# Attention in front of a squared-ReLU layer: another step order for the periods without conversions, and query and key loads taken from a list

## The chip, the cores and the metric

The kernel runs on one core of one Trainium2 chip. The metric is device time in microseconds (us) of one execution, as the median of several runs. Beside the runs there is one profiled execution with a trace of every instruction on TensorE (PE, its weight loads are PEld), VectorE (DVE), ScalarE (ACT), GpSimd (POOL) and the sequencer that issues most transfers (SP). Line numbers such as L453 are those of the kernel before.

## The reference

```python
scores = (q @ k.T) / 8                                # 8 batches, 8 heads, 576 x 576, head size 64
thresh = max(scores, axis=-1) - tau
scores = where(scores >= thresh, scores, -1e9)
attn   = exp(scores - max(scores)); attn = attn / (sum(attn) + 1e-9)
x      = (attn @ v) laid out as (8 * 576, 8 * 64)     # 4608 tokens x 512
h      = maximum(x @ w_in, 0)                         # 512 -> 2048
out    = (h * h) @ w_out                              # 2048 -> 512
```

`q`, `k`, `v` and `tau` are 32-bit floats. `w_in` and `w_out` arrive as 64-bit floats and are turned into 32-bit ones by the kernel itself, in integer arithmetic on ACT, POOL and DVE.

## The kernel before

**Stages.** The attention of all heads comes first (about the first 510 us of the span), then nine passes of the hidden layer, then the output layer. The two layers use a scheme of block sums (seven products for eight, twice nested), whose sums of weight blocks are made by POOL during the attention. The change touches the attention alone.

**Pairs, units and periods.** Two heads make a pair; there are 32 pairs. A unit is a block of 128 query rows of a pair (four per pair), or the last 64 rows of two pairs together; there are 144 units. A period p works on the two units A = 2p and B = 2p + 1 with their softmax; 72 periods hold the work and a few before and after fill and drain the pipeline. What belongs to one pair of units is spread over several periods, so that every engine has something to do.

**The steps** (names as in the order lists; `period`, L623, makes them):

- `T` transposes a pair's queries or keys on PE (L399); `eT` takes them out of PSUM on ACT (L404, L412) and then asks for the loads of a later pair (`ask_ahead`).
- `SA`, `SB` are the products of queries with 512 keys for units A and B (L435, 64x512), `RA`, `RB` the products with the last 64 keys (L435, 64x64).
- `topA0` to `topB1` find the row maxima of one head each on DVE and write the scores to SBUF (L453). `leastA`, `leastB` make the thresholds from them on POOL (L460). `powA0` to `powB1` are the exponentials on ACT (L463). `maskA0` to `maskB1` compare, multiply and sum on DVE (L468): two operands from SBUF, result to SBUF.
- `over` (POOL, L475) and `inv` (DVE, L478) make the inverse of the row sums; `Q` spreads it over 64 rows by small products on PE (L518).
- `V`, `W`, `U` transpose the weights of attention on PE (L381), nine chunks in three lots; `eV`, `eW`, `eU` take them out of PSUM on ACT (L526). `V` and `U` share one PSUM tile, `pt`; `W` and `Q` lie in two of the banks of `SB`.
- `PV` multiplies values with weights on PE (L535), into the banks that `SA` uses next. `x` takes the result out, half by ACT (L665), half by DVE (L667, in periods without conversions with the scaling). `xm` scales the other half on POOL (L677) and issues the stores of x (L581).
- `c1` to `c6` convert one chunk of weights, `fetch` loads one. `s1` and `s2` each take one step of a list of sums of weight blocks (and later of x for the first pass) on POOL: L122 or L125, one 128x512 operation, both inputs in SBUF.

**Orders.** An order is a string of step names, executed as program order by `run_period` (L731). A hyphen behind a name means that the step of the period before is meant, two hyphens of the one before that. Every engine executes its instructions in this order; semaphores alone tie the engines to each other. There are orders for periods 0 and 1 (`BEGIN_WITH`), one for the periods with conversions (`CONVERTING`, periods 2 to 34) and one for all others (`PLAIN`). `s1` acts from period 36 on, `s2` in periods 36 to 59 (its hyphen puts the instruction one period later).

**Order of one engine within a period without conversions, before** (lag within the pipeline left out):

- DVE: x, maskA0, then `inv`, then maskB0, topA0, topA1, maskB1, topB0, topB1, maskA1. In the trace's terms, from a first top: top, top, mask, top, top, mask, x, mask, inverse, mask.
- POOL: s2, xm, leastA, s1, leastB, over.

**Loads.** `load_q` issues two transfers of 128 KB for a pair, `load_k` seven smaller ones, all on SP (pair 0 in part on ACT). `ask_ahead` (L344) issues all of a pair's transfers at the place where `eT` stands, up to two pairs ahead. `load_v` issues one transfer per pair. `fetch` issues one transfer of 512 KB per chunk.

Of the kernel before, what the change touches and what calls it, by code (L numbers as in the profile page):

```python
# [48 lines left out]
def kernel(  # L49
# [25 lines left out]
    nc = tc.nc  # L75
    B, H, S, D = q.shape
    P = 128
# [212 lines left out]
    def load_q(i):  # L290
        b, hp = pairs[i]
        h = 2 * hp
        qn = sb.tile([P, FULL, P], FP32, tag="qn", bufs=2, name="qn")
        for j in range(2):
            nc.sync.dma_start(
                out=qn[:, :, ds(j * D, D)], in_=q[b, h + j, 0:MAIN, :].rearrange("(t p) d -> p t d", p=P)
            )
        loaded[i, 0] = qn

    def load_k(i):  # L300
        b, hp = pairs[i]
        h = 2 * hp
        kn = sb.tile([P, FULL, P], FP32, tag="kn", bufs=2, name="kn")
        rn = sb.tile([P, P], FP32, tag="rn", bufs=2, name="rn")
        for j in range(2):
            queue = nc.scalar if i == 0 and j == 0 else nc.sync
            keys = k[b, h + j, :, :].rearrange("(p c) d -> p c d", c=CH)
            for e in range(2):
                queue.dma_start(
                    out=kn[ds(e * HALF, HALF), :, ds(j * D, D)],  # L310
                    in_=keys[:, ds(e * FULL, FULL), :],
                )
# [3 lines left out]
            queue.dma_start(out=rn[REST:P, ds(j * D, D)], in_=keys[:, CH - 1, :])  # L316
        nc.sync.dma_start(
            out=rn[0:REST, :].rearrange("p (j d) -> p j d", j=2),
            in_=q[b, h : h + 2, MAIN:S, :].rearrange("j p d -> p j d"),
        )  # L320
        loaded[i, 1], loaded[i, 2] = kn, rn

    def load_v(i):
        b, hp = pairs[i]
# [66 lines left out]

    def turn(i, which, spots, other=None):

        nat, to = loaded.pop((i, which)), places(i)
        of = [nat[:, t, :] for t in range(FULL)] + ([loaded.pop((i, 2))] if which else [])
        for t, x in enumerate(of):
            for r, (spot, at) in enumerate(spots):
                rows = ds(r * HALF, HALF)
                made = nc.tensor.transpose(spot[:, ts(t, HALF)], x[rows, :], ident[rows, rows])  # L399
                touch("turns", made, at, BANK)  # L400
        half, kind = FULL * HALF, "turnedk" if which else "turnedq"

        def scaled(to, spot):
            touch(kind, nc.scalar.activation(out=to, in_=spot[0], func=AF.Identity, scale=qscale[:, :]), spot[1], BANK, i)  # L404
# [164 lines left out]
    def sums_due(p):  # L569

        return p > max(starts) + 2 and not converts(p)

    def sums_step():
        while summing and next(summing[0], 0) == 0:
            summing.popleft()

    def ask(every=True):

        while given:
            to, from_ = given.popleft()  # L580
# [11 lines left out]
    def begun(n):  # L592
        return starts.get(n)

    FIRST_PERIOD = -2
    PLAIN = """
        s2- PV-- x-- T-- V-- W-- c2 SA- c3- maskA0-- xm-- inv-- Q-- eT-- RB- maskB0-- topA0- c1- eV-- U-
        topA1- leastA- eW-- SB- powB1-- maskB1-- eU- RA topB0- c4 topB1- s1 powA1- leastB- maskA1- over- c5
        powA0- c6 powB0- fetch
    """.split()  # L600
    CONVERTING = """
        SB- c1 RA topB0- powA1- c2- topB1- PV- c5- powA0- maskA0- eT- leastB- over- V- x- T powB0- SA RB W-
        maskA1- c3 c4 inv- Q- c6- fetch topA0 eV- topA1 leastA U xm- maskB0- powB1- eW- eU maskB1- s1 s2
# [12 lines left out]

# [6 lines left out]
    def period(p):  # L623
# [48 lines left out]
        def given_out():  # L672
            if has(2 * m):
                x = late.pop("x")
                made = x[:, 0 : 1 + converts(p), :].rearrange("p j n -> p (j n)")
                scale = wT[m][:, ds(SCALE_AT * P, (1 + converts(p)) * P)]
                nc.gpsimd.tensor_tensor(out=made, in0=made, in1=scale, op=ALU.mult)  # L677
# [14 lines left out]
        def every(key):  # L692
# [13 lines left out]
            "s1": lambda: sums_due(p) and sums_step(), "s2": lambda: sums_due(p) and p < 60 and sums_step(), "fetch": lambda: fetch(begun(p + 2)),  # L706
            "next": lambda: fetch(begun(p + 3)),
        }
        steps["over"] = lambda: do(a, "over")
# [428 lines left out]
    with tc.manual_schedule():  # L1138
        with ExitStack() as stack:
            sc = stack.enter_context(tc.tile_pool(name="sc", bufs=1, space=PSUM)).tile([P, 6 * BANK], FP32, name="sc")  # L1140
            pt_pool = stack.enter_context(tc.tile_pool(name="pt", bufs=1, space=PSUM))

            def keep_busy(times, to=None):

                if to is None:
                    to = pt_pool.tile([P, 2, BANK], FP32, tag="pt", name="idle")[:, 0, 0:P]
                for _ in range(times):
                    nc.tensor.transpose(to, ident[:, :], ident[:, :])

            load_q(0)  # L1150
            load_k(0)
# [4 lines left out]
            ask_ahead(0, 1)  # L1156
            load_v(0)
# [204 lines left out]
```

## Time and profile before

| what | value |
|---|---|
| runs | 1315.05, 1312.97, 1312.98 us, median 1312.98 |
| profiled execution | 1310.12 us, span of its instructions 1308.3 us |
| PE busy | 1272.8 us (97% of the span) |
| DVE busy | 1015.0 us (78%) |
| ACT busy | 854.0 us (65%) |
| POOL busy | 1016.6 us (78%) |

The shares are means over three stages with different limits. In the page's 40 slices DVE is at nine tenths or more from the second slice to the fifteenth, and at five to eight tenths after the attention; ACT falls to two to six tenths there, and PE stays at nine tenths in nearly every slice. So what the attention costs is read from the attention's own stretch, and there from its two kinds of periods. A row of the trace's timeline gives start, duration, engine, line, operation, tiles and count; rows of one engine overlap where an instruction begins before the one ahead of it has drained, so that the step from start to start is what an instruction costs, and the duration is longer.

### The profile page before, as it was taken

To read this page: it belongs to the slowest core of one execution; us is meant where nothing else is said; L and a number is where in the kernel's file an instruction comes from. 1 tells how busy PE (TensorE), PEld (TensorE's weight loads), DVE (VectorE), ACT (ScalarE), POOL (GpSimd) and SP (SyncE) were. 2 spreads that over 40 slices of the span, in tenths; PEclk is the share of its full clock that TensorE was granted. 3 is DMA by queue.
4 is the path that set the end of the run, shared out by engine and by line. 5 is a ranking of instruction groups with operands and counts; after the bars stand their busy time and mean duration, and the time that the engine had idled before them with its cause. 6 is when DMAs were issued, how large, how long until landed. Compare 5 with 4: busy or idle time off the path is not lost.

```text
span 1308.3 us, 45977 instructions
## 1 busy us (share of the span) xinstructions
PE 1272.8 (97%) x18287; PEld 1104.7 (84%) x18287; DVE 1015.0 (78%) x2384; ACT 854.0 (65%) x1537; POOL 1016.6 (78%) x1070
## 2 busy tenths in 40 slices
PE   8999999999999999999999999999999999999998
PEld 5777766666666777988888888999999999999998
DVE  6999999999999996787886877867646654665463
ACT  6999999988888996576665866665524332433240
POOL 2999999887878652798897998858777777777775
PEclk8999999999999999999999999999999999999999
DMA  6555667443333322566767767779645234513511
GB/s 168 149 147 157 190 174 200 115 99 86 82 72 79 80 54 53 175 209 191 221 192 210 221 172 223 198 263 392 225 160 162 65 99 161 162 56 107 162 34 33
DMA packets 291415, 196.22 MB, mean 150 GB/s; under 512 B 100096, under 2 KB 252160, under 8 KB 291200
## 3 DMA queue, kind: packets, MB, share of 16 engines
q1 hardware_dynamic: 289888, 192.87, 50.9%
q8 instruction: 144, 2.36, 0.8%
q14 instruction: 71, 0.58, 0.1%
q10 hardware_dynamic: 1312, 0.41, 0.1%
HBM read 120.85 MB, written 72.35 MB: 148 GB/s over the span
## 4 chain that ended last, share of the span: by engine, by line
PE 71%; ACT 8%; DMA 6%; DVE 5%; issue 4%; POOL 4%; SPq 1%; DVEq 0%; POOLq 0%; ACTq 0%
PE po L1096 27%; PE ph L954 13%; PE ph L961 9%; PE sc L535 9%; PE sc L435 8%; ACT arena L526 3%; PE pt L381 2%; DVE arena L453 2%; ACT arena L463 2%; DMA g<-arena 2%; DMA arena<-xT 2%; DVE arena L468 1%; PE sc L399 1%; DVE arena L125 1%; DMA arena<-g 1%
## 5 line engine op out<-in xcount | busy, mean ns | idle before, releaser
L125 POOL TENSOR_TENSOR arena<-arena 128x512 f32<-128x512 f32 (+1 forms) x314 | 377.6, 1221 | 136.8 <-DVE arena L125 103.0
L1096 PE MATMUL po<-wall,arena 128*128 128x128 f32 x3528 | 395.1, 276 | 1.9 <-ACT arena L771 1.4
L1096 PEld LDWEIGHTS po<-wall,arena 128*128 128x128 f32 x3528 | 394.4, 192 | 2.5 <-ACT arena L771 1.8
L125 DVE TENSOR_TENSOR arena<-ph,arena 128x512 f32<-128x512 f32 x378 | 255.1, 689 | 78.8 <-PE ph L954 30.9
L122 POOL TENSOR_TENSOR arena<-arena 128x128 f32<-128x128 f32 (+1 forms) x322 | 264.8, 823 | 27.4 <-DMA arena<-w 11.6
L954 PE MATMUL ph<-arena,wall 128*128 128x256 f32 x1176 | 256.9, 381 | 3.1 <-DVE arena L125 2.7
L468 DVE SCALAR_TENSOR_TENSOR arena<-arena 128x576 f32<-128x576 f32 x288 | 256.4, 908 | 1.7 <-ACT arena L463 1.2
L954 PEld LDWEIGHTS ph<-arena,wall 128*128 128x128 f32 x1176 | 222.7, 190 | 37.0 <-DVE arena L125 7.9
L125 DVE TENSOR_TENSOR arena<-po,arena 128x128 f32<-128x128 f32 x378 | 108.3, 290 | 167.9 <-PE po L1096 163.6
L463 ACT ACTIVATE arena<-arena 128x576 f32<-128x576 f32 x288 | 215.6, 781 | 9.5 <-DVE arena L453 9.4
L810 ACT COPY c<-arena 128x512 f32<-128x512 f32 (+1 forms) x295 | 169.1, 578 | 74.5 <-DVE arena L122 35.8
L435 PE MATMUL sc<-arena 64*64 64x512 f32 (+1 forms) x2304 | 197.8, 423 | 16.8 <-DVE arena L453 8.6
L453 DVE TENSOR_SCALAR_CACHE_REDUCE arena<-sc 128x576 f32<-128x576 f32 x288 | 205.6, 750 | 8.8 <-PE sc L435 5.0
L460 POOL TENSOR_SCALAR arena<-arena,tau_p 128x2 f32<-128x2 f32 x144 | 102.2, 710 | 94.3 <-DVE arena L453 84.7
L122 DVE TENSOR_TENSOR arena<-arena,c 128x512 f32<-128x512 f32 x235 | 154.4, 666 | 13.3 <-ACT c L810 9.2
L535 PE MATMUL sc<-arena 64*64 64x128 f32 (+1 forms) x5760 | 163.0, 261 | 0.4 <-ACT arena L526 0.3
L435 PEld LDWEIGHTS sc<-arena 64*64 64x64 f32 x2304 | 75.7, 134 | 100.9 <-DVE arena L453 40.2
L526 ACT COPY arena<-pt 128x1024 f32<-128x1024 f32 x144 | 146.1, 1015 | 8.3 <-PE pt L381 7.7
L535 PEld LDWEIGHTS sc<-arena 64*64 64x64 f32 x5760 | 148.7, 134 | 1.4 <-ACT arena L526 0.7
L771 ACT COPY arena<-po 128x128 f32<-128x128 f32 x63 | 16.6, 264 | 186.4 <-PE po L1096 183.7
L961 PE MATMUL ph<-arena,wall 128*128 128x128 f32 x1176 | 132.0, 276 | 0.6 <-DVE arena L667 0.6
L961 PEld LDWEIGHTS ph<-arena,wall 128*128 128x128 f32 x1176 | 131.6, 192 | 0.9 <-issue 0.7
(54 smaller groups left out, 1153.6 us busy)
## 6 DMA issues: line engine op xcount, KB each, us to landing
arena<-g SPq DMA_DIRECT2D x144, 256.0 KB, 4.3
g<-arena SPq DMA_DIRECT2D x192, 128.0 KB, 2.9
w<-arena SPq DMA_DIRECT2D x60, 256.0 KB, 2.7
wall<-w SPq DMA_DIRECT2D x49, 256.0 KB, 5.2
g<-arena SPq DMA_DIRECT2D x48, 256.0 KB, 3.5
arena<-w SPq DMA_DIRECT2D x44, 256.0 KB, 3.3
arena<-in_v_dram SPq DMA_DIRECT2D x32, 288.0 KB, 4.1
out_dram<-arena SPq DMA_DIRECT2D x70, 128.0 KB, 2.8
```

What stands on the lines that cost most here:

```text
L122: e.tensor_tensor(out=out, in0=x, in1=y, op=ALU.subtract)
L125: e.tensor_tensor(out=out, in0=x, in1=y, op=ALU.add)
L435: made = nc.tensor.matmul(sc[at, ds(to, count)], lhs, kT[rows, ds(at_k, count)], start=True, stop=True)
L453: made = nc.vector.tensor_scalar(out=s[:, j, :], in0=sc[:, ds(at, S)], scalar1=1.0, scalar2=None, op0=ALU.mult, op1=ALU.min, accum_out=nmx ...
L463: nc.scalar.activation(out=w[:, :, j, :], in_=of(j), func=AF.Exp, bias=nmx[:, j : j + 1], scale=-1.0)
L468: nc.vector.scalar_tensor_tensor(out=w[:, :, j, :], in0=of(j), scalar=thr[:, j : j + 1], in1=w[:, :, j, :], op0=ALU.is_le, op1=ALU.mult, a ...
L526: touch("weights", nc.scalar.copy(joined(to), whole(pt, 0, count)), at, 2 * BANK, m)
L535: made = nc.tensor.matmul(sc[ds(u * D, D), ds(5 * j * BANK + row, count)], loaded_v[i][rows, (c - (u != j)) % CH, :], wT[m][rows, ds(weigh ...
L810: nc.scalar.copy(c, y)
L954: nc.tensor.matmul(to[:, 2 * j : 2 * j + 2, :], W_IN[m, k][:, ts(2 * h + j, P)], part_x(steps, k, m), start=(not more and j == 0), stop=Tr ...
L961: nc.tensor.matmul(to[:, j, :], W_IN[m, k][:, ts(j, P)], x, start=(not more and j == 0), stop=True, skip_group_check=True,)
L1096: nc.tensor.matmul(to, g[:, j, :], w[:, j, :], start=(not more and j == 0), stop=(j == 3), skip_group_check=True)
```

## The change

1. **A new `PLAIN` order.** The set of steps is the same, with `ahead` in front; the order and some lags differ.
2. **Query and key loads.** `load_q` and `load_k` become generators that yield after each transfer. `ask_ahead` appends them to a list `wanted`; the new step `ahead` issues three transfers from it (four in periods up to 1), and `given_out` (`xm`) issues two more, so five per period. `turn` takes from the list until its own pair's loads are out.
3. **Periods 0 and 1.** `ahead` is added. In period 1, `next`, which asks for the third chunk of weights, moves from the second place to the end.
4. `CONVERTING` gets `ahead` in front and is otherwise unchanged.

```diff
     def load_q(i):
         qn = sb.tile([P, FULL, P], FP32, tag="qn", bufs=2, name="qn")
+        loaded[i, 0] = qn
         for j in range(2):
-            nc.sync.dma_start(
+            yield nc.sync.dma_start(
...
     def ask_ahead(i, which):
         while asked[which] < min(len(pairs) - 1, i + (2 if i else 1)):
             asked[which] += 1
-            (load_k if which else load_q)(asked[which])
+            i_ = asked[which]
+            wanted.append((i_, which, (load_k if which else load_q)(i_)))
+
+    wanted = deque()
+
+    def ahead(count):
+        while wanted and count:
+            if next(wanted[0][2], 0) == 0:
+                wanted.popleft()
+            else:
+                count -= 1
...
     def turn(i, which, spots, other=None):
+        while any(x[0:2] == (i, which) for x in wanted):
+            ahead(1)
...
     PLAIN = """
-        s2- PV-- x-- T-- V-- W-- c2 SA- c3- maskA0-- xm-- inv-- Q-- eT-- RB- maskB0-- topA0- c1- eV-- U-
-        topA1- leastA- eW-- SB- powB1-- maskB1-- eU- RA topB0- c4 topB1- s1 powA1- leastB- maskA1- over- c5
-        powA0- c6 powB0- fetch
+        ahead PV-- RA- c2- c4- T- W-- U- c5- Q-- c1- maskB0-- x-- eT- SA- xm-- s1 maskB1-- RB- c3- eW-- SB-
+        eU- topA0- V- powA0- eV- topA1- topB0- topB1- powA1- powB0- over- leastA- powB1- inv- c6 maskA0- s2-
+        maskA1- leastB- fetch
     """.split()
...
     BEGIN_WITH = {
         0: """
-        SA RA RB SB fetch topA0 T topA1 leastA topB0 topB1 leastB powA0 powA1 eT powB0 powB1 maskA0 maskA1
-        maskB0 maskB1
+        SA RA RB SB fetch ahead topA0 T topA1 leastA topB0 topB1 leastB powA0 powA1 eT powB0 powB1 maskA0
+        maskA1 maskB0 maskB1
         """.split(),
         1: """
-        fetch next SA RA RB SB T eT over topA0 topA1 leastA inv V topB0 topB1 leastB powA0 powA1 eV W Q powB0 eW
-        maskA0 maskA1 powB1 maskB0 maskB1
+        fetch ahead SA RA RB SB T eT over topA0 topA1 leastA inv V topB0 topB1 leastB powA0 powA1 eV W Q
+        powB0 eW maskA0 maskA1 powB1 maskB0 maskB1 next
...
             ask(False)
+            ahead(2)
...
+            "ahead": lambda: ahead(3 if p > 1 else 4),
```

Engine by engine, a period of the new order from its first top on is, on DVE: topA0, topA1, topB0, topB1, inv, maskA0, maskA1, and then of the next period's list maskB0, x, maskB1. On POOL: over, leastA, s2, leastB, then xm, s1. On ACT: powA0, eV, powA1, powB0, powB1, then x, eT, eW, eU. On PE: SB, V, then PV, RA, T, W, U, Q, SA, RB. On SP at the start, the loads of the first two chunks now stand in front of the queries of pairs 2 and 3, and the third chunk behind them; before, the first chunk stood in front of these queries, and the second and third behind them.

More of the change, by code (lines that the diff above doesn't have):

```diff
@@ L293, in load_q @@
         qn = sb.tile([P, FULL, P], FP32, tag="qn", bufs=2, name="qn")
+        loaded[i, 0] = qn
         for j in range(2):
-            nc.sync.dma_start(
+            yield nc.sync.dma_start(
                 out=qn[:, :, ds(j * D, D)], in_=q[b, h + j, 0:MAIN, :].rearrange("(t p) d -> p t d", p=P)
             )
-        loaded[i, 0] = qn
     def load_k(i):
@@ L304, in load_k @@
         rn = sb.tile([P, P], FP32, tag="rn", bufs=2, name="rn")
+        loaded[i, 1], loaded[i, 2] = kn, rn
         for j in range(2):
@@ L308, in load_k @@
             for e in range(2):
-                queue.dma_start(
+                yield queue.dma_start(
                     out=kn[ds(e * HALF, HALF), :, ds(j * D, D)],
@@ L315, in load_k @@
                 nc.scalar.dma_start(out=tau_c[:, :], in_=wide)
-            queue.dma_start(out=rn[REST:P, ds(j * D, D)], in_=keys[:, CH - 1, :])
-        nc.sync.dma_start(
+            yield queue.dma_start(out=rn[REST:P, ds(j * D, D)], in_=keys[:, CH - 1, :])
+        yield nc.sync.dma_start(
             out=rn[0:REST, :].rearrange("p (j d) -> p j d", j=2),
@@ L320, in load_k @@
         )
-        loaded[i, 1], loaded[i, 2] = kn, rn
     def load_v(i):
@@ L596 @@
     PLAIN = """
-        s2- PV-- x-- T-- V-- W-- c2 SA- c3- maskA0-- xm-- inv-- Q-- eT-- RB- maskB0-- topA0- c1- eV-- U-
-        topA1- leastA- eW-- SB- powB1-- maskB1-- eU- RA topB0- c4 topB1- s1 powA1- leastB- maskA1- over- c5
-        powA0- c6 powB0- fetch
+        ahead PV-- RA- c2- c4- T- W-- U- c5- Q-- c1- maskB0-- x-- eT- SA- xm-- s1 maskB1-- RB- c3- eW-- SB-
+        eU- topA0- V- powA0- eV- topA1- topB0- topB1- powA1- powB0- over- leastA- powB1- inv- c6 maskA0- s2-
+        maskA1- leastB- fetch
     """.split()
     CONVERTING = """
-        SB- c1 RA topB0- powA1- c2- topB1- PV- c5- powA0- maskA0- eT- leastB- over- V- x- T powB0- SA RB W-
-        maskA1- c3 c4 inv- Q- c6- fetch topA0 eV- topA1 leastA U xm- maskB0- powB1- eW- eU maskB1- s1 s2
+        ahead SB- c1 RA topB0- powA1- c2- topB1- PV- c5- powA0- maskA0- eT- leastB- over- V- x- T powB0- SA
+        RB W- maskA1- c3 c4 inv- Q- c6- fetch topA0 eV- topA1 leastA U xm- maskB0- powB1- eW- eU maskB1- s1
+        s2
     """.split()
@@ L705, in period @@
             "c5": lambda: convert5(begun(p - 1)), "c6": lambda: convert6(begun(p - 1)),
-            "s1": lambda: sums_due(p) and sums_step(), "s2": lambda: sums_due(p) and p < 60 and sums_step(), "fetch": lambda: fetch(begun(p + 2)),
+            "s1": lambda: sums_due(p) and sums_step(), "s2": lambda: sums_due(p) and p < 60 and sums_step(), "ahead": lambda: ahead(3 if p > 1 else 4),
+            "fetch": lambda: fetch(begun(p + 2)),
             "next": lambda: fetch(begun(p + 3)),
@@ L1148, in keep_busy @@
                     nc.tensor.transpose(to, ident[:, :], ident[:, :])
-            load_q(0)
-            load_k(0)
+            for _ in load_q(0):
+                pass
+            for _ in load_k(0):
+                pass
             read_tau()
@@ L1156 @@
             ask_ahead(0, 1)
+            ahead(99)
             load_v(0)
```

## The prediction

> **What bounds the kernel now.** The page's shares are means over three stages, so I went to the windows of the two kinds of periods without conversions: with both sums of weight blocks (360 to 400 us) and after the second has ended (440 to 480). Columns: stretch, its length, busy us of PE, PEld, DVE, ACT, POOL, granted clock, DMA share, GB/s.
>
> ```profile
> 360.00:400.00 40.00, 37.62 (x980) 26.45 (x974) 39.43 (x103) 34.70 (x56) 32.04 (x34) 1.00 0.31 70
> 440.00:480.00 40.00, 39.99 (x1090) 30.42 (x1084) 39.31 (x113) 38.34 (x67) 23.81 (x31) 1.00 0.31 69
> ```
>
> DVE is busy for 98% of both. Yet the second stretch gets more done. The row maxima (four per period), by first and last start, tell the length of a period:
>
> ```profile
> L453 DVE TENSOR_SCALAR_CACHE_REDUCE arena<-sc x97: 745/746/750, 252.2 to 424.7; 128x576 f32<-128x576 f32 x97
> L453 DVE TENSOR_SCALAR_CACHE_REDUCE arena<-sc x49: 746/747/759, 424.7 to 501.3; 128x576 f32<-128x576 f32 x49
> ```
>
> The first 24 periods take (424.7 - 252.2) / 24 = 7.19 us each, the next 12 take (501.3 - 424.7) / 12 = 6.38. The timeline of DVE says why:
>
> ```profile
> 391.57 0.75 DVE L453 TENSOR_SCALAR_CACHE_REDUCE arena<-sc 128x576 f32<-128x576 f32 x1
> 392.25 0.08 DVE L453 DVE_READ_ACCUMULATOR arena<-sc 128x1 f32 x1
> 392.25 0.81 DVE L468 SCALAR_TENSOR_TENSOR arena<-arena 128x576 f32<-128x576 f32 x1
> 392.99 0.08 DVE L468 DVE_READ_ACCUMULATOR arena<-arena 128x1 f32 x1
> 392.99 0.28 DVE L667 TENSOR_TENSOR arena<-sc,arena 128x128 f32<-128x128 f32 x1
> 393.19 0.81 DVE L468 SCALAR_TENSOR_TENSOR arena<-arena 128x576 f32<-128x576 f32 x1
> 393.93 0.08 DVE L468 DVE_READ_ACCUMULATOR arena<-arena 128x1 f32 x1
> 394.12 0.18 DVE L478 RECIPROCAL arena<-arena 128x4 f32<-128x4 f32 x1
> 394.22 1.84 DVE L468 SCALAR_TENSOR_TENSOR arena<-arena 128x576 f32<-128x576 f32 x1
> 395.99 0.08 DVE L468 DVE_READ_ACCUMULATOR arena<-arena 128x1 f32 x1
> ```
>
> ```profile
> 391.09 1.28 POOL L122 TENSOR_TENSOR wall<-wall 128x512 f32<-128x512 f32 x1
> 392.43 0.79 POOL L460 TENSOR_SCALAR arena<-arena,tau_p 128x2 f32<-128x2 f32 x1
> 393.29 0.80 POOL L475 TENSOR_SCALAR arena<-arena 128x4 f32<-128x4 f32 x1
> 394.17 1.28 POOL L122 TENSOR_TENSOR wall<-wall 128x512 f32<-128x512 f32 x1
> ```
>
> Three masks (L468) take 0.81 us, the fourth 1.84: "busy", but standing still for 1.03 us, because POOL's sum `s2` began 0.05 us earlier. The mask ends at 396.06, so its own 0.81 begins at 395.25, 0.20 before the sum's end at 395.45. The sum at 391.09, `s1`, stands over row maxima, which read PSUM, and costs DVE nothing. The other way round, a sum that comes second waits: L460 and L475 take 0.8 behind a mask, while one with nothing in its way takes 0.29 (last row of the next fence). Where `s2` is gone, the small `xm` stands in its place and holds the same mask for 1.02 - 0.81 = 0.21:
>
> ```profile
> 462.04 0.46 POOL L677 TENSOR_TENSOR arena<-arena 128x128 f32<-128x128 f32 x1
> 462.09 1.02 DVE L468 SCALAR_TENSOR_TENSOR arena<-arena 128x576 f32<-128x576 f32 x1
> ```
>
> ```profile
> 16.39 0.29 POOL L460 TENSOR_SCALAR arena<-arena,tau_p 128x2 f32<-128x2 f32 x1 [1.13 <-DVE arena L478]
> ```
>
> That is the whole difference of the two kinds of periods: 7.19 - 6.38 = 0.81 = 1.03 - 0.21. The Trainium skill ("SBUF — State Buffer", section "Who interferes with whom") has the rule for it: a DVE instruction with two SBUF inputs and a GpSimd one that reads SBUF exclude each other for a whole instruction, and who issues first wins. The trace agrees.
>
> **The new order, part by part.** From start to start DVE's instructions cost: a maximum 0.68 (391.57 to 392.25), a mask 0.74 (392.25 to 392.99), `x` 0.20, the inverse 0.10 (394.12 to 394.22). Set a period's first maximum at 0. Maxima at 0, 0.68, 1.36, 2.04; inverse 2.72; maskA0 2.82, maskA1 3.56, maskB0 4.30, `x` 5.04, maskB1 5.24 to 5.98. So DVE's floor is 5.98, and what counts is who makes it wait. For the other engines I use ACT and PE where nothing holds them up:
>
> ```profile
> 457.70 1.00 ACT L526 COPY arena<-pt 128x1024 f32<-128x1024 f32 x1
> 458.60 2.11 ACT L463 ACTIVATE arena<-arena 128x576 f32<-128x576 f32 x3
> 460.61 0.26 ACT L665 COPY arena<-sc 128x128 f32<-128x128 f32 x1
> 461.02 0.84 ACT L404 ACTIVATE arena<-sc,qscale 128x256 f32<-128x256 f32 x2 [0.16 <-PE sc L399]
> ```
>
> ```profile
> 458.30 2.29 PE L535 MATMUL sc<-arena 64*64 64x64 f32 x106
> 460.53 0.46 PE L399 MATMUL sc<-ident,arena 64*128 64x64 f32 x8
> 460.82 0.66 PE L381 MATMUL pt<-ident,arena 64*128 64x64 f32 x16
> 461.32 0.29 PE L381 MATMUL sc<-ident,arena 64*128 64x64 f32 x4
> 461.54 1.09 PE L435 MATMUL sc<-arena 64*64 64x512 f32 x8
> 462.45 0.41 PE L518 MATMUL sc<-ident,arena 64*64 64x64 f32 x16
> 462.68 0.30 PE L435 MATMUL sc<-arena 64*64 64x64 f32 x8
> ```
>
> *ACT.* powA0 can start once the first maximum is out, at about 0.8; it costs 0.67 (2.01 / 3), eV 0.90, three more exponentials 2.01: `x` starts at 4.38 and ends near 4.65. Then eT 0.75 (the 0.84 of 461.02, less its drain), eW 0.5 (half of eV's elements, an estimate), eU 0.9 as eV: to 6.8, inside the next period, before the next powA0. In the second window ACT is busy 38.34 / 40 of 6.38 = 6.11 per period; that is its bound.
>
> *PE.* PV needs both A maxima out (1.36 + 0.1); it takes up to 2.2 (458.30 to 460.53, the longest kind of unit), mostly less, to about 3.6. RA 0.15, T 0.3, W 0.2, U 0.5, Q 0.23: to 5.0. SA's first head waits for ACT's `x` (4.65), its second for DVE's (5.04 + 0.28 = 5.32, plus 0.05). Half of SA is 0.45, then the first products of RB and their draining, 0.3 to 0.35. So the next first maximum can start at 5.37 + 0.45 + 0.3 = 6.12, or, if PE reaches SA only at 5.15, at 5.15 + 0.91 + 0.33 = 6.39. This wait is the new bound. Behind SA on PE stand RB, SB and V; SB is needed only at 1.36 of the next period and V's copy at 1.5, so they don't lengthen it.
>
> *POOL.* `s2` comes after leastA, which needs the second maximum (1.43): 1.55 + 0.29 = 1.84, then 1.28, to 3.12. A sum lets go 0.20 before its end, at 2.92; maskA0 wants to begin at 2.82. So `s2` lies under the B maxima and costs 0.1, where it cost 1.03. `xm` starts behind ACT's `x` at 4.7 and finds maskB0 (4.30 to 5.04) at work: it waits, and is through when maskB1 begins at 5.24, since DVE's `x` of 0.20 stands between and reads only one operand from SBUF. `s1` then comes after maskB1 has begun, waits for its end at 6.0 and runs under the A maxima. Its 1.28 ends near 7.2, 1.1 into the next period, before leastA needs POOL at 1.55.
>
> The engines' loops give 6.1 to 6.4. Turns (queries, keys or none) and PV (units of 128 rows or two halves) differ from period to period, and the longest of four loops counts each time, so I take **6.3**. Bounds of a working order: 6.1 (ACT's busy time) and 6.6 (PE's late case plus 0.2). Sum: 24 x (7.19 - 6.3) = 21.4 and 12 x (6.38 - 6.3) = 1.0 saved; by the bounds 30 and 11.
>
> *Loads at the start.* The second chunk of 512 KB now goes ahead of the queries for pair 2, which PE already waits for:
>
> ```profile
> 13.27 0.43 SPq L192 DMA_DIRECT2D arena<-in_moe_w_in_dram  x1
> 13.82 2.44 SPq L295 DMA_DIRECT2D arena<-in_q_dram  x4
> ```
>
> ```profile
> 19.49 0.69 PE L399 MATMUL sc<-ident,arena 64*128 64x64 f32 x8 [0.87 <-DMA arena<-in_q_dram]
> ```
>
> ```profile
> 15.00:20.00 5.00, 2.28 (x52) 1.79 (x51) 5.00 (x16) 4.34 (x7) 1.31 (x3) 0.91 1.12 290
> 20.00:25.00 5.00, 5.00 (x44) 2.28 (x44) 2.14 (x6) 2.01 (x4) 1.72 (x3) 0.50 0.82 234
> ```
>
> At 290 GB/s the chunk takes 0.52 MB / 290 = 1.8 us, and T with all behind it on PE (SA, RB, SB, PV) starts that much later. The granted clock is at half in the second row; of the later start a part comes back when the clock does, since less work is then done at half speed. I take 1.5 lost, between 0 and 4 (a longer time at half clock). That the third chunk is asked for behind the queries moves nothing on an engine: SP only issues it 0.5 us earlier or later. The Trainium skill ("TensorE: Matmul & The Clock Gate", Part 1) lets an idle window of some 3.4 us halve the clock; the trace fits, and by this rule the longer wait could cost a second such window, some 2 us more than my 1.5.
>
> *Loads while converting.* Five transfers per period from the list against nine per pair and 2.25 periods, four per period, needed: the list stays short, and a load asked for at one turn has 4.5 periods until its own. What could be gained is DVE's idle time in the 30 periods from 36.6 to 244.1 us, 0.7 + 2.7 us:
>
> ```profile
> L468 DVE SCALAR_TENSOR_TENSOR arena<-arena 128x576 f32<-128x576 f32 x120 | 93.1, 813 | 0.7 <-POOL arena L213 0.4 <-ACT arena L463 0.3
> L453 DVE TENSOR_SCALAR_CACHE_REDUCE arena<-sc 128x576 f32<-128x576 f32 x120 | 85.9, 752 | 2.7 <-issue 1.4 <-ACT arena L526 1.0
> ```
>
> I take 1 gained, between 3 gained and 3 lost (as much again, if a spread load stands in front of a chunk). The generators themselves are no instructions. Filling and draining between the orders: 0, within 2 either way.
>
> Sum: -21.4 - 1.0 + 1.5 - 1.0 = -21.9. Against the profiled execution's own 1310.12 us that is 1288.2. That execution was 2.86 us below the median of the runs shown (1312.98); from the median the sum gives 1291.1, and I say **1291**.
>
> **Rivals.**
>
> *POOL gets in first.* Place: maskB1. If DVE runs later than I have it by 0.4 us, so that maskB0 begins after 4.7, `xm` goes ahead of it, `s1` is in the queue when maskB0 ends, and takes the 0.20 of DVE's `x` to begin before maskB1. Then maskB1 stands for 1.28 - 0.20 - 0.20 = 0.9 or so, and the first maximum follows it directly: 5.98 + 0.1 + 0.9 + the delay of 0.4 that set it off = 7.4. Over 24 periods +5, then, until the sums run out (56 steps, eight of them behind the 24 periods), 8 x 0.8 = +6.4, and +1.5 at the start: about 1325. For it: the same engine pair did exactly this before. (The Trainium skill's rule above, by which the issue order alone decides, leaves it open.) Against it: a margin of 0.4 us, and ACT, which fixes `x`, follows the maxima just as DVE does.
>
> *PE is late.* PV, five transposes and products stand between the A maxima and SA, and any slip lands on the first maximum. At 6.8 per period: 24 x 0.39 = 9.4 saved, 12 x 0.42 = 5.0 lost, 1.5 lost at the start: 1310. For it: PE is busy 39.99 of 40 us in the second window. Against it: those ends are modelled, and its steps from start to start, with V (0.5), SB (0.91) and T, add up to about 6.1.
>
> *The order does what it should, and the start or the conversions take it back.* Loss of 4 + 3 + 2 against 22: 1300. That the order changes nothing at all would need `s2` to meet a mask for the full 1.03 again; its place under the B maxima excludes that unless leastA comes 0.9 late.
>
> **How the numbers follow.** The forecast as summed, 1282 to 1301: 0.72. PE late, 1301 to 1311: 0.12; it holds no change (0.2% is 2.6 us, about what a measurement of this kernel can tell) with 0.03 and faster with the rest. POOL first, wholly or in a good part of the periods, 1312 to 1327: 0.10. Start and conversions worse than bounded: 0.06, half of it slower. Faster 0.72 + 0.09 + 0.02 = 0.83, same 0.04, slower 0.13. The low end of the range is 30 saved and 1 gained (1282), the high end takes in most of the PE case (1309).
>
> **What would show it.** Right: masks of 0.81 to 0.95 us throughout 252 to 500 us, `s2` ending at about the start of maskA0, `xm` at 0.8 behind maskB0, a DVE gap of 0.1 to 0.4 us ahead of the first maximum with PE L435 as its end, 36 periods of 6.2 to 6.5, T of pair 2 near 21 us. Wrong: one mask in four at 1.6 or more (POOL first), or gaps ahead of the first maximum of 0.7 and more (PE late), or the first window at half clock twice as long.

## The result, and the profile after

| kernel | runs | median us | lowest to highest | profiled execution |
|---|---|---|---|---|
| before | 5 | 1312.98 | 1311.15 to 1315.64 | 1310.12, span 1308.3 |
| changed | 5 | 1303.65 | 1297.37 to 1305.76 | 1303.65, span 1301.5 |

The changed kernel takes 0.9913 of the time before, with a 95% interval of 0.9884 to 0.9943: it is 9 us faster, where 22 were forecast. In the changed kernel's profile lines have moved by 13 or 14: the row maxima are L466, the masks L481, `x` L679 on ACT and L681 on DVE, `xm` L691, the products of `SA` to `SB` L448.

First the stretches that the prediction began with, now of the changed kernel (same columns: stretch, length, busy us of PE, PEld, DVE, ACT, POOL, granted clock, DMA share, GB/s), and the row maxima of the 24 periods with both sums and of the 12 behind them, by first and last start:

```profile
360.00:400.00 40.00, 40.00 (x1070) 30.55 (x1066) 36.66 (x109) 36.74 (x64) 29.85 (x37) 1.00 0.38 89
440.00:480.00 40.00, 40.00 (x1050) 31.42 (x1046) 36.67 (x110) 36.59 (x63) 18.58 (x29) 1.00 0.24 53
```

```profile
L466 DVE TENSOR_SCALAR_CACHE_REDUCE arena<-sc x97: 746/752/759, 257.2 to 417.3; 128x576 f32<-128x576 f32 x97
L466 DVE TENSOR_SCALAR_CACHE_REDUCE arena<-sc x49: 751/752/759, 417.3 to 496.3; 128x576 f32<-128x576 f32 x49
```

The 24 periods now take (417.3 - 257.2) / 24 = 6.67 us each instead of 7.19. The 12 others take (496.3 - 417.3) / 12 = 6.58 instead of 6.38: they became longer. DVE, which was at 98% in both stretches, is at 92%. It waits again, in one place only. One period of its timeline, beginning behind the four maxima (which start at 397.28):

```profile
397.28 0.76 DVE L466 TENSOR_SCALAR_CACHE_REDUCE arena<-sc 128x576 f32<-128x576 f32 x1 [0.56 <-ACT arena L539]
...
400.00 0.17 DVE L491 RECIPROCAL arena<-arena 128x4 f32<-128x4 f32 x1
400.09 0.89 DVE L481 SCALAR_TENSOR_TENSOR arena<-arena 128x576 f32<-128x576 f32 x1
...
400.91 0.81 DVE L481 SCALAR_TENSOR_TENSOR arena<-arena 128x576 f32<-128x576 f32 x1
...
401.65 0.81 DVE L481 SCALAR_TENSOR_TENSOR arena<-arena 128x576 f32<-128x576 f32 x1
...
402.39 0.28 DVE L681 TENSOR_TENSOR arena<-sc,arena 128x128 f32<-128x128 f32 x1
402.59 0.80 DVE L481 SCALAR_TENSOR_TENSOR arena<-arena 128x576 f32<-128x576 f32 x1
...
403.96 0.76 DVE L466 TENSOR_SCALAR_CACHE_REDUCE arena<-sc 128x576 f32<-128x576 f32 x1 [0.56 <-issue]
```

No mask stands for 1.84 us any more: they take 0.89, 0.81, 0.81 and 0.80. The new wait is the 0.56 us ahead of the first maximum. The releasers named there ("ACT L539" in one period, "issue" in the next) can't be right: ACT's copies there are long done or still running when the maximum starts. POOL in the same period:

```profile
399.08 1.29 POOL L122 TENSOR_TENSOR wall<-wall 128x512 f32<-128x512 f32 x1
400.34 0.80 POOL L473 TENSOR_SCALAR arena<-arena,tau_p 128x2 f32<-128x2 f32 x1
402.09 0.68 POOL L691 TENSOR_TENSOR arena<-arena 128x128 f32<-128x128 f32 x1 [0.95 <-ACT arena L679]
402.74 1.80 POOL L122 TENSOR_TENSOR wall<-wall 128x512 f32<-128x512 f32 x1
```

`s2` (399.08 to 400.37) ends under the first mask and holds it by 0.89 - 0.80 = 0.09. `xm` at 402.09 waits behind the third mask. Its row ends at 402.77, 0.18 into the fourth mask, which isn't held by it (0.80). `s1`, at 402.74, finds that mask at work and waits for its end.

Between the two traces the span fell by 1308.3 - 1301.5 = 6.8 us. The table of stages under the experiments shows where it came from: 24 periods gave 12.4 us, 12 periods took 2.4 back, and start, conversions and filling took back a further 5 us, against 1.7 gained behind the start of the last of these periods. The medians differ by more, 9.3 us: the trace of before is of an execution 2.9 us below its median, that of the changed kernel of one at its median.

### The profile page after: what moved, and what is told of

Read it like the earlier page. It is cut to its first block, busy times and chain, and to the rows that moved or that the text cites. A ratio compares the mean times of both kernels' runs of the same rounds, so it can differ in the third digit from the quotient of the medians.

```text
span 1301.5 us, 46003 instructions
## 1 busy us (share of the span) xinstructions
PE 1275.3 (98%) x18287; PEld 1118.3 (86%) x18287; DVE 989.4 (76%) x2384; ACT 847.9 (65%) x1537; POOL 989.4 (76%) x1070
## 4 chain that ended last, share of the span: by engine, by line
PE 83%; ACT 8%; DMA 3%; issue 2%; POOL 2%; SPq 1%; DVE 1%; ACTq 0%; DVEq 0%; POOLq 0%
PE po L1112 29%; PE ph L970 15%; PE sc L548 11%; PE sc L448 10%; PE ph L977 10%; PE pt L392 4%; ACT arena L539 3%; ACT arena L476 2%; PE sc L531 1%; PE sc L412 1%; DMA arena<-in_q_dram 1%; DVE arena L125 1%; POOL arena L125 1%; DMA arena<-xT 1%; ACT c L826 1%
## 5 line engine op out<-in xcount | busy, mean ns | idle before, releaser
L122 POOL TENSOR_TENSOR arena<-arena 128x128 f32<-128x128 f32 (+1 forms) x322 | 270.0, 840 | 25.3 <-DMA arena<-w 9.4
L466 DVE TENSOR_SCALAR_CACHE_REDUCE arena<-sc 128x576 f32<-128x576 f32 x288 | 203.3, 752 | 31.5 <-issue 12.6
L481 DVE SCALAR_TENSOR_TENSOR arena<-arena 128x576 f32<-128x576 f32 x288 | 225.7, 820 | 1.3 <-ACT arena L476 1.3
L448 PE MATMUL sc<-arena 64*64 64x512 f32 (+1 forms) x2304 | 191.8, 417 | 7.1 <-ACT arena L679 1.9
L548 PEld LDWEIGHTS sc<-arena 64*64 64x64 f32 x5760 | 149.9, 134 | 3.6 <-ACT arena L539 0.9
L539 ACT COPY arena<-pt 128x1024 f32<-128x1024 f32 x144 | 147.1, 1022 | 6.9 <-PE pt L392 6.3
L448 PEld LDWEIGHTS sc<-arena 64*64 64x64 f32 x2304 | 88.6, 134 | 73.1 <-issue 44.4
L473 POOL TENSOR_SCALAR arena<-arena,tau_p 128x2 f32<-128x2 f32 x144 | 84.7, 588 | 78.2 <-DVE arena L466 57.0
```

The source lines that it names most:

```text
L122: e.tensor_tensor(out=out, in0=x, in1=y, op=ALU.subtract)
L448: made = nc.tensor.matmul(sc[at, ds(to, count)], lhs, kT[rows, ds(at_k, count)], start=True, stop=True)
L466: made = nc.vector.tensor_scalar(out=s[:, j, :], in0=sc[:, ds(at, S)], scalar1=1.0, scalar2=None, op0=ALU.mult, op1=ALU.min, accum_out=nmx ...
L481: nc.vector.scalar_tensor_tensor(out=w[:, :, j, :], in0=of(j), scalar=thr[:, j : j + 1], in1=w[:, :, j, :], op0=ALU.is_le, op1=ALU.mult, a ...
L539: touch("weights", nc.scalar.copy(joined(to), whole(pt, 0, count)), at, 2 * BANK, m)
L548: made = nc.tensor.matmul(sc[ds(u * D, D), ds(5 * j * BANK + row, count)], loaded_v[i][rows, (c - (u != j)) % CH, :], wT[m][rows, ds(weigh ...
```

## The experiments

The question was which of three things kept the gain at 9 us: the new order's own period, the new order of loads at the start, or the loads spread over the conversions. Times before, measured beside the kernels: 1313.77 us (first four kernels) and 1310.6 us (last three).

| kernel | median us | lowest to highest | ratio to before, 95% |
|---|---|---|---|
| the new order alone | 1302.22 | 1299.30 to 1305.23 | 0.9910 (0.9891 to 0.9929) |
| the loads alone | 1313.39 | 1310.46 to 1316.25 | 0.9998 (0.9985 to 1.0011) |
| `x` sooner | 1290.20 | 1286.98 to 1295.82 | 0.9826 (0.9804 to 0.9849) |
| queries first | 1299.48 | 1296.56 to 1300.22 | 0.9883 (0.9861 to 0.9905) |
| the old order with one sum | 1315.71 | one run | |
| both moves | 1287.98 | 1287.05 to 1288.92 | 0.9821 (0.9797 to 0.9846) |
| the changed kernel again | 1300.74 | 1298.88 to 1302.98 | 0.9920 (0.9892 to 0.9948) |

The stages, from the starts of the first maxima in each trace (us): the start up to period 4, then 30 periods with conversions (4 to 34), then the mean of the 24 periods with both sums (35 to 59) and of the next 12:

| kernel | period 4 at | 30 with conversions | each of 24 | each of 12 |
|---|---|---|---|---|
| before | 36.66 | 207.47 | 7.188 | 6.381 |
| changed | 37.53 | 210.84 | 6.671 | 6.582 |
| changed, again | 39.72 | 209.84 | 6.674 | 6.583 |
| order alone | 36.35 | 212.08 | 6.670 | 6.612 |
| loads alone | 38.66 | 209.09 | 7.201 | 6.383 |
| `x` sooner | 39.36 | 207.24 | 6.375 | 6.293 |
| queries first | 36.00 | 207.37 | 6.671 | 6.582 |
| old order, one sum | 36.68 | 212.77 | 6.397 | 6.383 |
| both moves | 36.07 | 209.65 | 6.356 | 6.325 |

### The new order alone

The kernel before, with nothing but the new `PLAIN` (without `ahead`):

```diff
     PLAIN = """
-        s2- PV-- x-- T-- V-- W-- c2 SA- c3- maskA0-- xm-- inv-- Q-- eT-- RB- maskB0-- topA0- c1- eV-- U-
-        topA1- leastA- eW-- SB- powB1-- maskB1-- eU- RA topB0- c4 topB1- s1 powA1- leastB- maskA1- over- c5
-        powA0- c6 powB0- fetch
+        PV-- RA- c2- c4- T- W-- U- c5- Q-- c1- maskB0-- x-- eT- SA- xm-- s1 maskB1-- RB- c3- eW-- SB-
+        eU- topA0- V- powA0- eV- topA1- topB0- topB1- powA1- powB0- over- leastA- powB1- inv- c6 maskA0- s2-
+        maskA1- leastB- fetch
     """.split()
```

> The kernel before with the new PLAIN order and nothing else of the change: loads as before, issued where eT stands, third chunk asked for as before. Theory (the new order saves about 12 us in the 24 long periods, loses about 2.4 in the 12 short ones, and the loads cost the rest): the start and the conversions are those of before (first maximum of period 3 near 30 us, period 35 entered near 252 to 253 us), periods of 6.67 and 6.57 us after that, 1300 us, so 3 to 4 us faster than the changed kernel's 1303.65. Rival (the slower conversions of the changed kernel are chance of a run): the time is that of the changed kernel within 1.5 us.

Measured: 1302.22 us, 0.9910, as good as the changed kernel itself. Its maxima give the same periods, (417.3 - 257.3) / 24 = 6.67:

```profile
L453 DVE TENSOR_SCALAR_CACHE_REDUCE arena<-sc x97: 746/752/759, 257.3 to 417.3; 128x576 f32<-128x576 f32 x97
```

So the whole gain is the order's, as far as these intervals tell. But its 30 periods with conversions took 212.08 us, 4.6 more than before, though up to period 34 this kernel's instructions are those of before. The waits of these periods (who waited, for whom: us in all, times, longest) name ACT's step of the conversion, waiting for the chunk's transfer:

```profile
ACT arena L206 <- DMA arena<-in_moe_w_out_dram: 4.0, 5, 1.2
...
ACT arena L206 <- DMA arena<-in_moe_w_in_dram: 2.5, 3, 1.3
```

In the trace of before the same two were 1.6 and 0.4 us, so 4.5 us of waiting came on top; that they make up all of the 4.6 isn't shown. The same instructions thus take 207.47 us in one execution, 212.08 here, and 212.77 in the old order with one sum below. So the expectation, 1300 us with the conversions of before, didn't come true, the rival did, and the changed kernel's 210.84 needs no explanation by its list of loads.

### The loads alone

The changed kernel, with the old `PLAIN` behind `ahead`:

```diff
     PLAIN = """
-        ahead PV-- RA- c2- c4- T- W-- U- c5- Q-- c1- maskB0-- x-- eT- SA- xm-- s1 maskB1-- RB- c3- eW-- SB-
-        eU- topA0- V- powA0- eV- topA1- topB0- topB1- powA1- powB0- over- leastA- powB1- inv- c6 maskA0- s2-
-        maskA1- leastB- fetch
+        ahead s2- PV-- x-- T-- V-- W-- c2 SA- c3- maskA0-- xm-- inv-- Q-- eT-- RB- maskB0-- topA0- c1- eV-- U-
+        topA1- leastA- eW-- SB- powB1-- maskB1-- eU- RA topB0- c4 topB1- s1 powA1- leastB- maskA1- over- c5
+        powA0- c6 powB0- fetch
     """.split()
```

> The changed kernel with the PLAIN order of before (ahead in front of it): loads from the list, third chunk asked for later. Theory: the queries of pair 2 come 1.7 us later than before at 21.2 us, and conversions wait for late keys and chunks: slower than before by 3 to 5 us (1316 to 1318); periods without conversions 7.19 and 6.38. Rival (chance, or the loads help): 1311 to 1313.

Measured: 0.9998, with an interval of 0.9985 to 1.0011: from 2 us gained to 1.4 lost. The 3 to 5 us lost that were expected didn't come. Its periods without conversions are those of before (7.20 and 6.38). The loads as a whole are worth nothing that this comparison can tell. Its start is 2 us later than before; whether something in the conversions gives that back can't be told from spreads of this size.

### `x` sooner

The changed kernel with two names of the order exchanged. DVE takes `x` out ahead of maskB0 instead of behind it:

```diff
-        ahead PV-- RA- c2- c4- T- W-- U- c5- Q-- c1- maskB0-- x-- eT- SA- xm-- s1 maskB1-- RB- c3- eW-- SB-
+        ahead PV-- RA- c2- c4- T- W-- U- c5- Q-- c1- x-- maskB0-- eT- SA- xm-- s1 maskB1-- RB- c3- eW-- SB-
```

> The changed kernel with x in front of maskB0 in PLAIN instead of behind it, so that DVE gives bank 5 free 0.74 us sooner. Theory (the 0.56 us gap of DVE ahead of each first maximum is the chain from the end of DVE's x over the whole of SA's second head, 1.07 us, and RB): SA starts both heads together behind Q, the gap falls to 0.1 to 0.3, periods become 6.25 to 6.35 us, 36 of them save 10 to 13 us: 1291 to 1294. Rival 1 (PE is late anyway, its own work from the A maxima to RB sets the period): periods stay above 6.5, less than 3 us saved. Rival 2 (xm now waits across two masks back to back and s1 gets in front of maskB1): one mask in four at 1.5 us or more, periods of 7 and over, slower than the changed kernel.

Measured: 1290.20 us, 13.5 less than the changed kernel by the medians and 11.4 by the two ratios to before, 0.9826 and 0.9913. The periods fall to (408.4 - 255.4) / 24 = 6.38 and (483.9 - 408.4) / 12 = 6.29:

```profile
L466 DVE TENSOR_SCALAR_CACHE_REDUCE arena<-sc x97: 745/752/759, 255.4 to 408.4; 128x576 f32<-128x576 f32 x97
L466 DVE TENSOR_SCALAR_CACHE_REDUCE arena<-sc x49: 744/752/758, 408.4 to 483.9; 128x576 f32<-128x576 f32 x49
```

This shows what the 0.56 us hung on: the way from DVE's `x`, through the products of `SA` and `RB`, to the first maximum. `x` comes sooner by a mask (0.74), and DVE's idle time ahead of the first maximum falls from 0.56 to 0.07 in the mean of the 24 periods and 0.10 of the 12 (0.16 in the period shown here). Another thing is seen in the timeline of DVE and POOL:

```profile
457.25 0.28 DVE L681 TENSOR_TENSOR arena<-sc,arena 128x128 f32<-128x128 f32 x1
457.45 0.80 DVE L481 SCALAR_TENSOR_TENSOR arena<-arena 128x576 f32<-128x576 f32 x1
...
457.74 0.83 POOL L691 TENSOR_TENSOR arena<-arena 128x128 f32<-128x128 f32 x1 [1.01 <-ACT arena L679]
...
458.18 1.00 DVE L481 SCALAR_TENSOR_TENSOR arena<-arena 128x576 f32<-128x576 f32 x1
...
459.34 0.76 DVE L466 TENSOR_SCALAR_CACHE_REDUCE arena<-sc 128x576 f32<-128x576 f32 x1
```

The two masks now stand back to back, with no `x` between them. `xm` waits behind the first, gets in ahead of the second, and the second takes 1.00 instead of 0.81. It costs 0.19, and the period is still 0.30 shorter than in the changed kernel (0.29 in the 12 short ones): 0.49 less idle time and 0.19 lost on the mask. `x` isn't what PE waits for here: in all 36 periods `SA` starts behind the end of `x`, by 0.14 to 0.79 us. Whether PE's own work ahead of `SA` or DVE's masks set the 6.3 us that are left wasn't tested.

### Queries first

The changed kernel with the order of two steps in period 1 exchanged, so that the queries of pair 2 go out ahead of the second chunk again:

```diff
-        fetch ahead SA RA RB SB T eT over topA0 topA1 leastA inv V topB0 topB1 leastB powA0 powA1 eV W Q
+        ahead fetch SA RA RB SB T eT over topA0 topA1 leastA inv V topB0 topB1 leastB powA0 powA1 eV W Q
```

> The changed kernel with ahead in front of fetch in period 1, so that the queries of pair 2 are issued before the second chunk, as in the kernel before. Theory (the second chunk in front of them is what delays the turn of pair 2 from 19.5 to 21.2 us): the turn starts at 19.4 to 19.7 us again, the maximum of period 3 at 30 us instead of 30.8, and 0.5 to 1.5 us are saved (1302 to 1303). Rival (the clock at half speed sets the start either way): the turn comes sooner, and the time stays.

Measured: 1299.48 us, against 1303.65 and 1300.74 in the two sets of the changed kernel: 1.3 to 4.2 us better by the medians and 4 to 5 by the ratios to before (0.9883 against 0.9913 and 0.9920), with intervals that overlap. The traces tell more than the medians. `T` of pair 2, first in the changed kernel, then here:

```profile
21.20 0.69 PE L412 MATMUL sc<-ident,arena 64*128 64x64 f32 x8 [2.58 <-DMA arena<-in_q_dram]
```

```profile
20.07 0.69 PE L412 MATMUL sc<-ident,arena 64*128 64x64 f32 x8 [0.61 <-DMA arena<-in_q_dram]
```

In the four traces with the chunk first, period 4's first maximum comes at 37.53, 39.72, 39.36 and 38.66 (mean 38.8), in the five with these queries first (before, the order alone, this kernel, and the old order with one sum and both moves below) at 36.66, 36.35, 36.00, 36.68 and 36.07 (mean 36.4). That is 2.5 us of the start, by the unrounded means, and the two groups don't overlap. Nor do the starts of `T`: 21.20 to 23.16 in the first, 19.49 to 20.24 in the second (19.4 to 19.7 was expected of this kernel, 20.07 came).

### The old order with one sum

The kernel before, in which `s2` never acts; the sums that are left over are made at the end of the attention, in one lump:

```diff
-            "s1": lambda: sums_due(p) and sums_step(), "s2": lambda: sums_due(p) and p < 60 and sums_step(), "fetch": lambda: fetch(begun(p + 2)),
+            "s1": lambda: sums_due(p) and sums_step(), "s2": lambda: sums_due(p) and p < 0 and sums_step(), "fetch": lambda: fetch(begun(p + 2)),
```

> The kernel before with s2 doing nothing: s1 alone takes the sums, one per period, and what is left of them is done at the end of the attention (so its total says little; the periods count). Theory (the 1.03 us standing mask is s2 alone, and xm takes its place at 0.21): all periods 36 to 71 are 6.38 us, the first 24 too, and the fourth mask is 1.0 us in each. Rival (the long mask has another cause in those periods, as the loads or the stage): 7.19 stays, or something between.

Its whole time, 1315.71 us in one run, says nothing on the order, since the sums come late. Its periods do: (411.1 - 257.6) / 24 = 6.40, and the mask that stood for 1.84 takes 1.02, behind an `xm` that began 0.05 sooner:

```profile
L453 DVE TENSOR_SCALAR_CACHE_REDUCE arena<-sc x97: 744/747/759, 257.6 to 411.1; 128x576 f32<-128x576 f32 x97
```

```profile
288.46 0.46 POOL L677 TENSOR_TENSOR arena<-arena 128x128 f32<-128x128 f32 x1
```

```profile
288.51 1.02 DVE L468 SCALAR_TENSOR_TENSOR arena<-arena 128x576 f32<-128x576 f32 x1
```

So the difference of the long and the short periods before was `s2` alone, and the old order without the collision has periods as short as the new one with `x` sooner (6.40 and 6.38), though with one sum in each instead of two.

### Both moves, and the changed kernel again

Both exchanges in one kernel:

```diff
-        ahead PV-- RA- c2- c4- T- W-- U- c5- Q-- c1- maskB0-- x-- eT- SA- xm-- s1 maskB1-- RB- c3- eW-- SB-
+        ahead PV-- RA- c2- c4- T- W-- U- c5- Q-- c1- x-- maskB0-- eT- SA- xm-- s1 maskB1-- RB- c3- eW-- SB-
...
-        fetch ahead SA RA RB SB T eT over topA0 topA1 leastA inv V topB0 topB1 leastB powA0 powA1 eV W Q
+        ahead fetch SA RA RB SB T eT over topA0 topA1 leastA inv V topB0 topB1 leastB powA0 powA1 eV W Q
```

> The changed kernel with x in front of maskB0 and with ahead in front of fetch in period 1. Theory (the two act in different stretches and add up): periods of 6.3 as in x_sooner, the turn of pair 2 near 19.5 us, 1287 to 1289.5, that is 1 to 2.5 us under x_sooner's 1290.2. Rival (the gain of the earlier queries is lost to chance in the conversions): 1290 to 1292.

Measured: 1287.98 us, 0.9821 of before, 22.6 us under the 1310.6 measured beside it. That is the lowest median here, but `x` sooner alone had 0.9826 in a set in which before took 1313.77 us, and the intervals overlap almost wholly. The 1 to 2.5 us expected of the queries' move would be 0.0008 to 0.0019 of the time, so whether it adds anything to `x` sooner isn't shown. In the traces period 4 comes 3.3 us earlier (36.07 against 39.36), and the conversions take 2.4 us more (209.65 against 207.24).

The changed kernel without an edit, to see how far its stages vary:

> The changed kernel once more, for the stretch from period 4 to period 34. Theory (how long the conversions take is chance of a run, as the same instructions took 207.5 us before and 212.1 with the order alone): a length other than 210.8 by more than 1 us, and a median within 3 us of 1303.65. Rival (the list of loads costs 3.4 us there): 210 to 211.5 again.

Measured: 1300.74 us, 0.9920. Its periods without conversions agree with the first trace to 0.003 us; its conversions took 209.84 us instead of 210.84, its start 2.2 us more. A length of 209.84 lies between what the theory and what the rival expected, so this run alone doesn't decide about the conversions; the kernels with the same instructions there, 207.47 to 212.77 above, do. The periods are fixed by the order; start and conversions vary from execution to execution.

## Why the prediction was right and wrong

**The stall and its end: right.** `s2` and a mask excluded each other, and without `s2` the old order's long periods fall from 7.19 to 6.40. In the new order `s2` lies under the maxima and the first mask, and costs 0.09 where 0.1 was forecast. Of POOL's small steps behind a mask, L473 takes 0.80 and `xm` 0.68, where 0.8 was forecast of `xm`.

**POOL gets in first: didn't come.** The fourth mask takes 0.80 in the changed kernel, for the reason given: `xm` gets its turn while DVE's `x` runs, and `s1` comes too late. With that `x` moved away, `xm` does get in, but it is a short one.

**The step that failed is "Half of SA is 0.45", in the wait for DVE's `x`.** The path was named rightly, and its first parts fit: in the period above `x` starts at 402.39 - 397.28 = 5.11 (forecast 5.04, plus the 0.1 of `s2`). But from its end, 402.67, to the first maximum at 403.96 pass 1.29 us, where 0.05 + 0.45 + 0.3 = 0.8 were forecast. The 0.45 was half of eight products of 0.91 in all, as if the two heads followed each other. Cut into very short windows around one `SA` (and the first products behind it), the timeline of the changed kernel shows what runs at one time; each row joins products that overlap:

```profile
442.21 0.60 PE L448 MATMUL sc<-arena 64*64 64x512 f32 x2
...
442.46 1.07 PE L448 MATMUL sc<-arena 64*64 64x512 f32 x6
```

```profile
442.13 0.28 DVE L681 TENSOR_TENSOR arena<-sc,arena 128x128 f32<-128x128 f32 x1
...
443.70 0.76 DVE L466 TENSOR_SCALAR_CACHE_REDUCE arena<-sc 128x576 f32<-128x576 f32 x1 [0.56 <-ACT arena L539]
```

The two heads use two halves of PE's rows, and run beside each other. The first head's first two products start at 442.21, the second head's at 442.46, 0.05 behind the end of `x` at 442.41. Each head passes its 512 columns twice. The second head's passes start at 442.46 and 442.94 and the small products of `RB` behind them at 443.37: 0.48 + 0.43 = 0.91 us for one head, as long as the prediction's rows have it for both. From there to the maximum at 443.70 it is 0.33, as forecast. So the term is 0.91 and not 0.45, 0.46 more. The forecast's own earliest point was 6.12; with 0.46 more it is 6.58, and most of the 12 periods measure 6.575 (mean 6.582). The 24 others, with the 0.1 of `s2`, measure 6.671 in the mean. That the wait hangs on `x` is shown by moving `x`; that it is the second head's passes which fill it is read from the times of single products, and these are the same in all 36 periods of this trace: `RB`'s last products start 0.96 us behind the end of `x` (0.05 and 0.91), and the maximum 1.29 behind it. When `SA`'s first head starts makes no difference. Here are the two periods at the ends of the range:

```profile
355.35 2.28 PE L448 MATMUL sc<-arena 64*64 64x512 f32 x22
...
355.68 0.28 DVE L681 TENSOR_TENSOR arena<-sc,arena 128x128 f32<-128x128 f32 x1
...
357.25 0.76 DVE L466 TENSOR_SCALAR_CACHE_REDUCE arena<-sc 128x576 f32<-128x576 f32 x1 [0.56 <-ACT arena L539]
```

```profile
369.03 0.28 DVE L681 TENSOR_TENSOR arena<-sc,arena 128x128 f32<-128x128 f32 x1
...
369.32 1.66 PE L448 MATMUL sc<-arena 64*64 64x512 f32 x20
...
370.60 0.76 DVE L466 TENSOR_SCALAR_CACHE_REDUCE arena<-sc 128x576 f32<-128x576 f32 x1 [0.56 <-ACT arena L539]
```

The first head starts 0.61 us ahead of the end of `x` in the one and 0.01 behind it in the other, and both times the maximum comes 1.29 behind that end.

With the periods as measured the sum changes as follows: 24 x (7.188 - 6.671) = 12.4 saved instead of 21.4, and 12 x (6.582 - 6.381) = 2.4 lost instead of 1.0 saved. Both errors together are 12.4 us, about the whole distance from 1291.1 to 1303.65. The second rival (PE late, 6.8 per period) came near in its time, 1310 against 1303.65, but not in its cause: `SA` starts its first head at 442.21, before `x` has ended at 442.41, so what stands ahead of `SA` on PE did not set the wait; the 36 periods above say the same.

That the time fell inside the stated 1282 to 1309 is in part luck. The forecast as summed was to come out between 1282 and 1301; 1303.65 lies in the part kept for the second rival, which had a chance of 0.12 and didn't happen. Nor did the signs of being right come: the gap is 0.56 where 0.1 to 0.4 was forecast, and the periods are 6.58 to 6.67 where 6.2 to 6.5 was. From trace to trace the fall is 6.8 us against 21.9: 12.4 of the difference are the periods, and 2.7 the start, the conversions, the filling and what follows the last period.

**The start: right in its mechanism, its size a little small.** `T` of pair 2 came at 21.20 (forecast near 21). The loss was put at 1.5 us between 0 and 4; the first trace has 0.87 (37.53 against 36.66), and the two groups of traces differ by 2.5. By the Trainium skill ("TensorE: Matmul & The Clock Gate", Part 1) the clock falls to half after an idle window of about 3.4 us, and the prediction drew from it that the longer wait could bring a second such window. In the changed kernel's first trace that window didn't come; when it was run again it did. The windows of that second trace (clock is the third value from the end):

```profile
20.00:25.00 5.00, 1.83 (x16) 1.08 (x20) 0.83 (x2) 0.72 (x2) 0.61 (x1) 0.50 0.93 240
25.00:30.00 5.00, 5.00 (x96) 3.21 (x92) 2.60 (x7) 2.93 (x5) 1.89 (x2) 0.67 0.32 67
```

There `T` came at 23.16 and the clock was still below full behind 25 us, at 0.67, where the first trace has 0.91:

```profile
25.00:30.00 5.00, 5.00 (x124) 3.59 (x126) 3.82 (x12) 4.89 (x10) 3.54 (x5) 0.91 0.31 69
```

Of the four traces with the chunk first, three have this longer stretch at half clock (0.64 to 0.72 in that row), of the five others none (0.91 to 1.00). So what the prediction drew from that rule came in three of four. The wait for the queries alone doesn't decide it: it was 2.58 us in the trace without the longer stretch, and 1.64 in one with it (the loads alone). Nor was PE idle all through the window ahead of the half clock, as the prediction's "the trace fits" would have it. In the trace of before it was busy for 1.12 of these 3.4 us:

```profile
15.70:19.10 3.40, 1.12 (x28) 0.78 (x28) 3.40 (x10) 3.40 (x6) 1.08 (x2) 1.00 1.18 284
19.10:25.90 6.80, 6.41 (x70) 3.64 (x74) 3.43 (x11) 3.81 (x7) 2.54 (x3) 0.50 0.77 213
```

**The conversions: no gain shown.** The forecast was 1 us gained, between 3 gained and 3 lost. The loads alone measure nothing, and the lengths of this stage spread by 3.6 us among the six traces with the list (207.24 to 210.84) and by 5.3 among the three without it (207.47 to 212.77). With the list ACT waits 1.5 to 2.5 us for chunks in all, without it 2.0, 5.2 and 6.5; from so few traces a small gain is neither shown nor excluded. One way in which an execution becomes longer can be seen in the changed kernel's trace: ACT's step on a chunk that arrived late, PE's wait behind it, and the windows around that:

```profile
165.94 0.69 ACT L206 ACTIVATE arena<-arena 128x512 f32<-128x512 f32 x1 [1.74 <-DMA arena<-in_moe_w_out_dram]
```

```profile
168.97 2.25 PE L448 MATMUL sc<-arena 64*64 64x512 f32 x16 [1.95 <-ACT arena L679]
```

```profile
167.50:169.20 1.70, 0.23 (x4) 0.23 (x8) 1.13 (x3) 1.70 (x7) 1.57 (x3) 1.00 0.92 242
169.20:172.70 3.50, 3.50 (x46) 2.41 (x44) 3.38 (x9) 2.45 (x4) 0.78 (x1) 0.51 0.88 240
```

Behind a transfer that is 1.74 us late PE has nothing to do for 1.95 us, and the next 3.5 us run at a clock of 0.51. The stretch of 30 periods is 3.4 us longer than before in this execution. Not every such wait brings the half clock with it: in the hidden layer of the order alone, PE waits for 2.27 us, and the clock stays full behind it.

```profile
622.34 3.94 PE L954 MATMUL ph<-arena,wall 128*128 128x256 f32 x17 [2.27 <-DVE arena L125]
```

```profile
622.40:632.00 9.60, 9.60 (x45) 8.42 (x46) 8.23 (x13) 3.36 (x7) 6.75 (x10) 1.00 0.68 190
```

**Filling.** From the order with conversions to the other one period takes 0.7 us more than before (8.82 instead of 8.10, the time from the first maximum of period 34 to that of 35), inside the 2 either way.

## What to carry to other kernels

When two engines hand work to and fro, cost the way from the last input to the first output in full: work that runs side by side on the parts of an engine takes its full time even when one part alone is waited for, so half of a group is not half of its time. In an order written by hand, put the step that another engine's long chain waits for ahead of work that nobody waits for; here one exchange of two names was worth about as much as the whole new order (0.0087 of the time each). A step that collides on a shared resource is best told by taking it away and looking at the period's length, not at the whole time.

## What the runs showed of the hardware

A POOL operation that waits behind a mask is served before the next mask, though that one stands directly behind in DVE's queue: 1.00 instead of 0.81 us for the second of two adjoining masks, in `x` sooner. The products of the two heads, 64 rows each on two halves of PE, take 0.91 us from their first start to that of the products behind them, the second head by itself (442.46 to 443.37, the first being 0.25 us ahead of it) as well as both together (461.54 to 462.45 in the trace of before). And a wait of PE of 1.95 us was followed by 3.5 us at half clock, though another of 2.27 us was followed by none.
